# Eight 128 KB weight loads issued in other steps of a linear-attention front end on one core

## The chip, the cores and the metric

The kernel runs on one core of a Trainium2 chip. A core has TensorE (PE in the profile, with its weight loads as PEld), VectorE (DVE), ScalarE (ACT), GpSimd (POOL) and SyncE (SP), and 16 DMA engines that all transfers share. The metric is the device time of one execution in microseconds (us), lower is better; times here are medians over a few executions.

## The reference, cut to what matters

A decayed linear attention over four batches of 768 rows, 8 heads of 64, is followed by a low-rank mixer over the rows and a two-layer feed-forward block.

```python
for b in range(nb):                      # blocks of 64 rows
    intra = np.einsum('bhic,bhjc->bhij', qb, kb) * Dmask[None]
    intra = np.einsum('bhij,bhjd->bhid', intra, vb)
    inter = np.einsum('bhid,bhde->bhie', qb * lam_pow[None], kv_state)
    out[:, :, sl] = intra + inter
    kv_state = lam_block[None, :, None, None] * kv_state + np.einsum('bhsd,bhse->bhde', kb_dec, vb)
# x: the attention output as (batch, row, 512)
h = x.transpose(0, 2, 1) @ U @ V                    # rank 32, over the 768 rows
u = x + h.transpose(0, 2, 1)
out = u + np.maximum(u @ w_ch1, 0.0) @ w_ch2        # 512 -> 2048 -> 512
```

The mixer's weights (U, V, w_ch1, w_ch2) arrive as 64-bit floats. The kernel loads them as pairs of 32-bit words and turns them into 32-bit floats itself.

## The kernel before, in words

**Stages.** The attention takes rows in 24 steps of 128 (NS = 24; six steps, NT = 6, make a batch). After it the first feed-forward product runs over 16 column tiles of w_ch1, and then the second product. Order on every engine is the order in which the code issues, since the whole front part is written out by hand under a manual schedule (L811-L851): for each step s the list `pieces` (L698-L732) names what is issued, and the loop at L838 issues it.

**A step of the attention.** In step s TensorE turns the q and k of step s+1 (`prep`, L416), multiplies the masked scores with v (`intra`, L514), updates the state (`state`, L486), adds the old state's share (`inter`, L525) and makes the scores of step s+1 (`scores`, L463), into which the mixer of an earlier batch is woven (`mix`, L618, and `turn`, L675). ScalarE copies q and k out of PSUM (L422), copies the output (`inter`, L531), scales the state (L456) and splits (L689). VectorE masks the scores (`masked`, L472), adds the mixer's output (`mixed`, L630), splits (L690) and writes the new state (L492, L494, L497). GpSimd scales q and k (L447, L436) and subtracts (L682). At the end of each batch (steps 5, 11, 17) `low` (L541) makes the low-rank product, and in the step after it, the turn of the batch (6, 12, 18), ScalarE and GpSimd split it (L584, L585) and SP exchanges parts of it with four 32 KB transfers (`other`, L595), on which the next `mix` waits.

**Queues.** SP issues the loads of q (in `prep`) and of k (`next_k`), the stores of u (`store`, L646) and the exchange L595; ScalarE issues the loads of v (`next_v`). SP's order in a step is: q load, in a turn of a batch L595 four times, then what `aside` issues, then the store, then the k load. A queue issues in order. The program gives its transfers eight completion semaphores in rotation, over SP's and ScalarE's queues alike, so each issue also waits for the landing of the transfer issued eight earlier.

**The steps of a weight.** `weight_steps` (L133) makes a list of small steps for one weight tile, and `aside(s)` (L800) issues those that a table sets at step s, ahead of `masked(s+1)`. For a tile of w_ch1 loaded in parts (`w1_steps(ft, True, True)`, L221) there are twelve: four fetches, each a 128 KB DMA on SP (L149; 128 rows of 1 KB); `one` (VectorE L170 on all four parts, with two ScalarE operations, L177 and L178, put off to the next step by `on_scalar`); the mantissa (L158); `two` (L188); `three` (L196, which needs L178); `four` (L201); `five` (ScalarE L231); `six` (L234); `seven` (L239). Steps set at NS run after the attention. The converted tiles 0 and 1 are the weights of the first products right behind the attention (L889, L900).

Of the kernel before, what the change touches and what calls it, by code (L numbers as in the profile page):

```python
# [18 lines left out]
def kernel(  # L19
# [40 lines left out]
    NS = B * NT  # L60
# [28 lines left out]
    def on_scalar(what):  # L89
        if late and late[0] is None:  # L90
            late.append(what)
        else:
            what()
# [115 lines left out]
    def plain(keep, key, tag="wf"):  # L209

        def dst():
            if key not in keep:
                keep[key] = (
                    tmp("wg") if tag == "tmp" else
                    plain_pool[-1].tile(
                        [P, C], FP32, tag=tag, bufs=1 if len(plain_pool) == 1 else 3, name="wf"
                    )
                )
            return keep[key]

        return dst  # L221
# [3 lines left out]
    def w1_steps(ft, in_parts=False, apart=False):  # L225
        st = {}

        def five():
            w1v[ft] = o = w_tile(ft)
            st["t"], st["p"] = o[:, 0, :].bitcast(FP32), w1_plain[ft]  # L230
            on_scalar(lambda: nc.scalar.mul(o[:, 0, :], st["p"], NEAR))  # L231

        def six():
            nc.vector.tensor_tensor(  # L234
                out=w1v[ft][:, 1, :], in0=st["p"], in1=st["t"], op=ALU.subtract
            )

        def seven():
            nc.vector.scalar_tensor_tensor(  # L239
                w1v[ft][:, 2, :], st["t"], -E, w1v[ft][:, 1, :].bitcast(FP32), ALU.mult, ALU.add  # L240
            )

        cols = moe_w_ch1[:, ft * P : (ft + 1) * P].rearrange("(c p) f -> p c f", p=P)
        return weight_steps(plain(w1_plain, ft), cols, C, in_parts=in_parts, apart=apart) + [
            five, six, seven,
        ]
# [47 lines left out]
    def w_tile(n):  # L294
        pool = more_w[0] if n > 1 and (n - 2) % 5 < 2 else w1_pool
        return pool.tile([P, 3, C], F32R, tag="w1", name="w1")
# [451 lines left out]
    def v_steps():  # L748

        st = {}  # L750

        def dst():
            if "v" not in st:
                st["v"] = wconv.tile([P, C], FP32, tag="wf", name="vf")[0 : 2 * R, 0:SH]
            return st["v"]

        def parts(gs):
            for half in range(2):
                rows, cols = slice(half * R, (half + 1) * R), slice(half * SH, (half + 1) * SH)
                for g in gs:  # L760
                    yield v_hl[g * R : (g + 1) * R, cols], rows

        def five():
            st["t"] = t = wconv.tile([P, C], FP32, tag="wt", name="vt")[0 : 2 * R, 0:SH]
            nc.vector.tensor_scalar(
                t.bitcast(U32), st["v"].bitcast(U32), HI, None, ALU.bitwise_and
            )
            on_scalar(high)

        def high():  # L770
            for out, rows in parts((0, 2)):
                nc.scalar.copy(out, st["t"][rows])

        def low(g, engine):
            for out, rows in parts((g,)):
                engine.tensor_tensor(
                    out=out, in0=st["v"][rows], in1=st["t"][rows], op=ALU.subtract
                )

        halves = [moe_V[:, half * SH : (half + 1) * SH] for half in range(2)]  # L780
        return weight_steps(dst, halves, SH, 2 * R, in_parts=True) + [
            five, lambda: low(1, nc.vector), lambda: low(3, nc.gpsimd),
        ]
# [6 lines left out]
    for steps, at in (  # L790
        (u_side, (-1, 1, 1, 2, 2)),
        (v_steps(), (0, 0, 3, 3, 4, 4, 4, 5, 5)),
        (w1_steps(0, True, True), (8, 9, 10, 11, 12, 14, 15, 16, 17, 17, 20, 21)),
        (w1_steps(1, True, True), (14, 15, 16, 17, 18, 22, 23, NS, NS, NS, NS, NS)),
    ):
        assert len(steps) == len(at)
        for step, n in zip(steps, at):
            side.setdefault(n, []).append(step)
# [695 lines left out]
```

## Time and profile before

| what | value |
|---|---|
| median of 3 runs | 641.93 us (641.23 to 645.38) |
| the profiled execution's own time | 642.39 us |
| its span, first to last instruction | 640.6 us |
| granted TensorE clock | 0.999 |
| attention, from the first scores to the first L889 product | 6.5 to 115.4 us |
| DMA queues, bytes in the whole span | q1 (SP) 121.53 MB, q10 (ScalarE) 6.42 MB, q8 (instructions) 0.67 MB |

The profile shows one execution. Times in it count from the start of the span. "Share" in a DMA column is the mean busy share of the 16 DMA engines; it can pass 1, as packets of one engine overlap. In the chain that ended last, "issue" is time in which the engine waited for nothing that the profile shows. A row of the timeline gives the start, the duration, the engine, the line and operation, the tiles written and read, and in brackets the idle time before it with what ended it.

### The profile page before, as it was taken

What the parts mean: (1) busy time and instruction counts of PE and PEld (TensorE: products, weight loads), DVE (VectorE), ACT (ScalarE), POOL (GpSimd) and SP (SyncE); (2) the same over time, 40 slices, a digit from 0 to 9 for tenths busy, and PEclk for the clock granted to TensorE, in tenths of its full rate; (3) what the DMA queues carried; (4) which work ended last, traced back from release to release, by engine and by line L of the source; (5) the groups of instructions that cost most, each with busy time, mean ns of one, the idle gap of its engine ahead of it and who ended that gap; (6) DMA issues with size and microseconds to landing.
All of it is one profiled execution on the core that took longest, in us unless ns stands there. A gap on an engine that the chain in (4) does not pass through costs nothing.

```text
span 640.6 us, 13612 instructions
## 1 busy us (share of the span) xinstructions
PE 631.0 (98%) x5203; PEld 530.8 (83%) x5203; DVE 459.5 (72%) x731; ACT 335.1 (52%) x614; POOL 146.4 (23%) x124
## 2 busy tenths in 40 slices
PE   9999989999999999999999999999999999999997
PEld 8889989888888888888888878888888888888886
DVE  6766867757878788788678799785574755855854
ACT  3776757445777777877777745232322322323220
POOL 4475968100000000000377600030120300300300
PEclk9999999999999999999999999999999999999999
DMA  9989996347888798765477786463363363543521
GB/s 218 252 205 266 225 245 161 135 171 269 310 288 273 271 322 290 252 208 202 160 258 231 243 310 222 134 226 99 103 227 98 117 205 100 179 140 99 181 83 65
DMA packets 141379, 128.83 MB, mean 201 GB/s; under 512 B 82498, under 2 KB 99394, under 8 KB 141314
## 3 DMA queue, kind: packets, MB, share of 16 engines
q1 hardware_dynamic: 116192, 121.53, 59.3%
q10 hardware_dynamic: 25122, 6.42, 4.4%
q8 instruction: 41, 0.67, 0.4%
q14 instruction: 24, 0.20, 0.1%
HBM read 78.64 MB, written 48.89 MB: 199 GB/s over the span
## 4 chain that ended last, share of the span: by engine, by line
PE 96%; DMA 2%; DVE 1%; issue 1%; ACT 1%; ACTq 0%; DVEq 0%
PE pz L959 25%; PE pz L1336 14%; PE pz L1334 14%; PE pd L1338 13%; PE z L959 4%; PE pss L463 4%; PE px L514 4%; PE p L959 3%; PE pz L889 2%; PE d L959 2%; PE px L525 2%; PE pqk L416 2%; PE c L959 1%; PE pkv L486 1%; PE pd L900 1%; PE pm L618 1%
## 5 line engine op out<-in xcount | busy, mean ns | idle before, releaser
L1318 ACT ACTIVATE m<-rm 128x512 fp32r<-128x512 f32 x96 | 60.6, 632 | 174.4 <-PE pd L1338 134.2
L1319 DVE SCALAR_TENSOR_TENSOR m<-rm,m 128x512 fp32r<-128x512 f32 x96 | 71.6, 747 | 81.7 <-ACT m L1318 81.7
L959 PE MATMUL pz<-u_hl,w 128*128 128x512 f32 x448 | 110.3, 389 | 0.0
L1334 PE MATMUL pz<-w_hl,m 128*128 128x512 f32 x264 | 102.7, 389 | 0.0
L1336 PE MATMUL pz<-w_hl,m 128*128 128x512 f32 x264 | 102.7, 389 | 0.0
L1338 PE MATMUL pd<-w_d,m 128*128 128x512 f32 (+1 forms) x267 | 101.4, 387 | 0.0
L959 PEld LDWEIGHTS pz<-u_hl,w 128*128 128x128 f32 x448 | 84.1, 188 | 17.5
L285 POOL TENSOR_TENSOR w<-w 128x512 fp32r<-128x512 f32 (+1 forms) x28 | 40.2, 1451 | 213.7 <-DVE w L279 194.3
L1320 DVE SCALAR_TENSOR_TENSOR m<-m 128x512 fp32r<-128x512 f32 x96 | 74.8, 779 | 3.0
L1366 POOL TENSOR_TENSOR o<-o,u 128x512 f32<-128x512 f32 x20 | 29.8, 1517 | 198.9 <-DVE o L1362 198.9
L959 PE MATMUL pz<-u_d,w 128*128 128x512 f32 x224 | 59.7, 389 | 0.0
L1338 PEld LDWEIGHTS pd<-w_d,m 128*128 128x128 f32 x267 | 49.8, 188 | 10.3
L1334 PEld LDWEIGHTS pz<-w_hl,m 128*128 128x128 f32 x264 | 49.6, 188 | 10.4
L1336 PEld LDWEIGHTS pz<-w_hl,m 128*128 128x128 f32 x264 | 49.6, 188 | 10.2
L959 PEld LDWEIGHTS pz<-u_d,w 128*128 128x128 f32 x224 | 42.0, 188 | 8.7
L966 ACT ACTIVATE pz<-pz 128x512 f32<-128x512 f32 x60 | 34.9, 581 | 26.6 <-PE pz L959 26.6
L1336 PE MATMUL pz<-w,m 128*128 128x512 f32 x120 | 46.7, 389 | 0.0
L1334 PE MATMUL pz<-w,m 128*128 128x512 f32 x120 | 46.7, 389 | 0.0
L1338 PE MATMUL pd<-w,m 128*128 128x512 f32 x120 | 46.7, 389 | 0.0
L472 DVE TENSOR_TENSOR sm<-pss,mask 128x512 f32<-128x512 f32 x48 | 30.9, 686 | 20.4 <-PE pss L463 20.4
L970 ACT ACTIVATE r<-pz 128x512 f32<-128x512 f32 x60 | 35.7, 596 | 14.2 <-PE pz L959 12.8
L196 DVE SCALAR_TENSOR_TENSOR sc<-words,sc 128x512 uint32<-128x512 uint32 (+2 forms) x34 | 24.7, 726 | 21.0 <-ACT sc L178 21.0
(144 smaller groups left out, 1112.3 us busy)
## 6 DMA issues: line engine op xcount, KB each, us to landing
r_d<-r SPq DMA_DIRECT2D x96, 256.0 KB, 2.9
rm<-r_d SPq DMA_DIRECT2D x96, 256.0 KB, 2.6
words<-in_moe_w_ch_dram SPq DMA_DIRECT2D x30, 512.0 KB, 4.6
wf<-forms_d SPq DMA_DIRECT2D x53, 128.0 KB, 2.8
u_d<-x_nat SPq DMA_DIRECT2D x24, 256.0 KB, 4.1
u<-u_d SPq DMA_DIRECT2D x24, 256.0 KB, 4.6
qraw<-in_q_dram SPq DMA_DIRECT2D x23, 256.0 KB, 4.8
out_dram<-o SPq DMA_DIRECT2D x23, 256.0 KB, 2.0
```

Of the source, the lines that this page charges most:

```text
L285: engine.tensor_tensor(out=st["third"], in0=st["low"].bitcast(FP32), in1=st["hi"].bitcast(FP32), op=ALU.subtract,)
L472: nc.vector.tensor_tensor(out=sm[:, x], in0=pss[:, x], in1=mask[:, x], op=ALU.mult)
L959: nc.tensor.matmul(out=out, lhsT=weights, rhs=moving, start=start and i == 0, stop=i == len(pieces) - 1, skip_group_check=not start,)
L966: nc.scalar.mul(acc, acc, 1.0 + E)
L970: nc.scalar.mul(r, acc, 4096.0)
L1318: nc.scalar.activation(out=m[:, 0], in_=r, func=AF.Relu, scale=NEAR)
L1319: nc.vector.scalar_tensor_tensor(m[:, 1], r, 0.0, hi, ALU.max, ALU.subtract)
L1320: nc.vector.scalar_tensor_tensor(m[:, 2], hi, E, low, ALU.mult, ALU.subtract)
L1334: nc.tensor.matmul(out=pz, lhsT=m[:, 0, cols], rhs=hi, start=first, stop=False)
L1336: nc.tensor.matmul(out=pz, lhsT=m[:, 1, cols], rhs=low, start=False, stop=end)
L1338: nc.tensor.matmul(out=pd[:, part], lhsT=m[:, 2, cols], rhs=third[:, part], start=first, stop=end, skip_group_check=part.stop != C,)
L1366: nc.gpsimd.tensor_tensor(out=o, in0=o, in1=u, op=ALU.add)
```

## The change

Two rows of the table that sets the steps of tiles 0 and 1 of w_ch1 are changed; nothing else.

```diff
-        (w1_steps(0, True, True), (8, 9, 10, 11, 12, 14, 15, 16, 17, 17, 20, 21)),
-        (w1_steps(1, True, True), (14, 15, 16, 17, 18, 22, 23, NS, NS, NS, NS, NS)),
+        (w1_steps(0, True, True), (6, 7, 11, 12, 13, 14, 15, 16, 17, 17, 20, 21)),
+        (w1_steps(1, True, True), (13, 18, 19, 20, 21, 22, 23, NS, NS, NS, NS, NS)),
```

Tile 0: the four fetches move from steps 8, 9, 10, 11 to 6, 7, 11, 12, and `one` from 12 to 13. Tile 1: the fetches move from 14, 15, 16, 17 to 13, 18, 19, 20, and `one` from 18 to 21. The other steps stay, with the two ScalarE operations of `one` following it, to steps 14 and 22. The number of instructions of every engine is the same (429 rows of SP, 646 of VectorE, 489 of ScalarE in both programs); TensorE's and GpSimd's order is the same throughout.

## The prediction

> **What bounds the kernel now.** I read the page first, then the chain of work that ended last, then the busy time of each engine step by step, then the timelines of SP, VectorE and ScalarE around the steps that change. TensorE is busy nearly all the time, so a word load costs or saves something only where it makes TensorE stop.
>
> ```profile
> PE 631.0 (98%) x5203; PEld 530.8 (83%) x5203; DVE 459.5 (72%) x731; ACT 335.1 (52%) x614; POOL 146.4 (23%) x124
> ```
>
> The chain runs through TensorE's own work from 37.05 to 115.4 us, with these stops in the steps concerned:
>
> ```profile
> 81.34 0.27 PE px L525 x6
> 81.61 0.91 issue
> ...
> 91.67 0.77 issue
> ...
> 106.43 0.41 issue
> ```
>
> The first two lie in steps 16 and 18, inside and just behind the four steps (14 to 17) that load words now; the third, in step 21, does not. TensorE waits there for nothing that the profile shows. The DMA part of the page for 79 to 83 us has one 16 KB packet of the instruction queue, about one per 256 instructions over the whole span (41 packets, 0.67 MB, two times 5203 TensorE instructions). I take these stops to be late instruction packets; that is an inference.
>
> The busy time in stretches that each begin with the scores of a step (issued at the end of the step before) has as its last two columns the DMA share and GB/s. Below are the stretches from the scores of step 13, right behind a turn of a batch; of 15 and 16, with words; of 19, behind the next turn; and of 21.
>
> ```profile
> 63.90:69.13 5.23, 5.04 (x130) 4.62 (x131) 3.69 (x9) 4.97 (x11) 4.92 (x7) 1.00 0.65 152
> ...
> 73.34:77.65 4.31, 4.31 (x125) 4.07 (x125) 4.08 (x7) 3.12 (x8) 4.31 (x4) 1.00 1.10 280
> 77.65:83.19 5.54, 4.63 (x127) 4.29 (x126) 4.16 (x7) 3.06 (x8) 3.87 (x4) 1.00 1.02 258
> ...
> 93.24:98.04 4.80, 4.70 (x129) 4.46 (x130) 3.50 (x9) 4.30 (x8) 4.65 (x6) 1.00 0.68 170
> ...
> 102.25:107.30 5.05, 4.63 (x127) 4.29 (x126) 4.69 (x7) 3.17 (x8) 5.05 (x5) 1.00 0.67 180
> ```
>
> The DMA engines are full in an ordinary step and two thirds full around the turns and in the last steps. The change moves words from full steps to emptier ones. Where it is tight is the turn at step 12: first SP, then VectorE.
>
> ```profile
> 64.11 2.80 SPq L595 DMA_DIRECT2D vp<-vp  x4
> 67.00 0.68 SPq L646 DMA_DIRECT2D u_d<-x_nat  x1
> ```
>
> ```profile
> 69.17 0.69 DVE L630 TENSOR_TENSOR x_nat<-pm,x_nat 128x512 f32<-128x512 f32 x1 [0.64 <-PE pm L618]
> 70.06 1.29 DVE L472 TENSOR_TENSOR sm<-pss,mask 128x512 f32<-128x512 f32 x2 [0.20 <-PE pss L463]
> ```
>
> The last words of tile 0 go out between the two SP rows, at about 66.95. `one`, which needs them, now stands between the two VectorE rows, ahead of the mask that TensorE waits for.
>
> **The change part by part.** No instruction is added or removed; every cost is of place. The sum is against the profiled execution: span 640.6 and 1.8 around it, 642.39 us, which is 0.46 above the median of 641.93.
>
> *Words leave steps 8 to 10 and 14 to 17.* What can go is the 0.91 and the 0.77. The bounds are nothing (the packets are late anyway, as in step 21) and the whole 1.68. If only the packets come sooner, the next things are late. At 81.61: ScalarE waited 3.13 us before its output copy at 84.08, because the v load ahead of it was held till 83.61 by a q load (issued 76.27, with words at 73.28 and 77.13 around it). The copy of k of that step ended at 85.86 + 0.59 = 86.45, and the scores that need it began at 86.92: 0.47 of the 0.91 is to be had even with ScalarE as late as now, and more if q lands sooner. At 91.67: the mix at 97.53 needs the last L595 transfer, issued at 94.98 and landed 2.2 later, at 97.2, so 0.35 of the 0.77. These two give 0.82. I take 1.0, nearer to 0.82 than to 1.68.
>
> *`one` of tile 0 behind the turn.* The words go out at 66.95. When do they land? The eight word loads of before took 4.5 to 7.2 us, all in full steps. In this lull 256 KB of v (issued 63.94) took 3.2 and the last 32 KB of L595 took 2.2. By 3.2 they land at 70.15; VectorE is ready at 69.86, so it waits 0.3. `one` took 0.61 and 0.42 before. The mask then begins at 70.57 to 70.76 instead of 70.06, and its first half (0.69) is done at 71.26 to 71.45. TensorE took it up at 71.17 in the chain, so it loses 0.1 to 0.3. Lower bound 0 (landing by 69.6); upper bound by the slowest row, 66.95 + 7.2 + 0.61 + 0.69 - 71.17 = 4.3. I take 0.3, since the v row is from the same lull. Behind `one` on VectorE stand the mask, the split and the new state, all of which TensorE needs within the step.
>
> *`one` of tile 1 at step 21.* The last words go out behind the k load of 99.19, at about 100.6. By 7.2 they are there at 107.8, by the median of 5.4 at 106.0. VectorE reaches `one` behind L239, at 107.19, and its mask waits for TensorE until 108.44, an idle time of 1.24 that holds the 0.42. Nothing, unless the slowest row holds: then 107.8 + 0.6 against 108.44, still nothing.
>
> *ScalarE's two operations (0.73 + 0.72) move from steps 13 and 19 to 14 and 22.* In step 14 ScalarE waits 1.19 before its output copy at 73.53; 0.26 is left over, and its k copy ends at 76.64 against scores at 77.65. In step 22 it waits 1.08 before 111.62, and the 0.37 left over ends the copy at 112.6, ahead of the products that write px again at 113.54. Nothing in both; without those waits it would be 1.45 each.
>
> *SP and what it is moved past.* In the new steps the store, the k load and the next q load go out later by one word issue, 0.38 in a lull (at 117.17) and up to 2.41 in a full step. The tightest reader is GpSimd's k scaling, which waited 0.57 and 1.39 for k at 82.38 and 86.06, in steps with words. Behind step 12, k landed at 73.0 and is read at 74.00, so 1.0 of slack takes the 0.4 to 0.7. In steps 18 to 20 the q loads have ended or are about to, and GpSimd has no work on the last k. No exchange is moved: all four L595 stand ahead of the words. In the other direction, in steps 8 to 10 and 14 to 17 a transfer that waits for the one eight earlier finds it two steps back instead of 1.6. I take 0.1 for all of this, between 0 and 0.9 (as much as the first stop).
>
> Sum: -1.0 + 0.3 + 0.1 = -0.6, so 641.8 for an execution like the profiled one, and 641.93 - 0.6 = 641.3 for a median of the kind shown.
>
> **What the Trainium skill says against it.** The instruction queue is served beside the full data queues, and the stops came with DMA shares of 1.02 and 1.09. The Trainium skill, "DMA: Bandwidth & Descriptors", section "Queues, rings and completion order", says that each DMA engine goes round between the queue rows it has work for, packet by packet. By that, an instruction packet does not stand behind the words in SP's row, and moving them would not bring it sooner. The trace agrees so far as rows share: from 79 to 83 us the ScalarE queue took 27.9% beside SP's 77.1%. What an instruction packet waits for, no row of before shows. What it would give is the second rival below.
>
> **The rivals.**
>
> 1. *Forecast: the stops shrink, VectorE waits a little.* 641.3. For it: both long stops are in the word steps 14 to 18, the new places have shares of 0.65 to 0.68. Against it: steps 8 to 11 load words at shares of 0.97 to 1.14 and show no stop over 0.1.
> 2. *The stops stay.* They are a matter of when TensorE crosses into a new block, and come back at other steps. Then 641.93 + 0.3 + 0.1 = 642.3. For it: the stop of 0.41 in step 21, with no words near, and steps 8 to 11 without any.
> 3. *Slower: VectorE's wait behind the turn decides.* Place: `one` in step 13. Every us by which the words land after 69.9 delays the mask, and from about 70.1 TensorE with it. By the fastest old row, 4.5, they land at 71.45; TensorE then gets its mask at 71.45 + 0.5 + 0.69 = 72.6, 1.5 late; by the median 5.4, 2.4 late. With the gain of 1.0 that is 641.93 - 1.0 + 1.5 to 2.4 + 0.1 = 642.5 to 643.4, and slower than before from a landing of about 70.9 on. Against it: the DMA share of 0.65 and the 3.2 of v.
> 4. *Everything goes: all three stops (2.09), no wait.* 639.8.
>
> **How the numbers follow.** The forecast has 0.45, the second rival 0.25, the third 0.2, the fourth 0.1. The predicted time is 641.3. Three of the executions shown lie within 1.2 us of each other and one 3.5 above; so I put about 1 us around the cases. From 640.0 (short of the fourth) to 643.6 (the third by the median row) leaves out 2 in 10. For the likeliest alone it is 640.5 to 642.3. One per cent is 6.4 us, about what a measurement of this kernel can tell from no change. The idle time of TensorE in all stretches from 37.05 to 115.40 us adds up to 2.8, so no gain of that size can be had here, and a loss of that size takes the third rival's upper bound of 4.3 in more than one place. Faster by over 1% 0.01, within 1% 0.97, slower by over 1% 0.02.
>
> **What would show it.** Right: the chain has no issue row near 0.8 in steps 14 to 18; VectorE's L170 in step 13 shows an idle time of some 0.3 before it that ends with the words' landing; the step from the scores of 14 to those of 15 keeps about 4.2 to 4.5 us; words issued in step 12 land in about 3 us. Wrong: issue rows of the same sum elsewhere (second rival), or L170 in step 13 idle for over 1 us with L514 behind it late (third). I would also be wrong if the moved words brought a stop to steps 18 to 21, where I count only 0.1.

## The result, and the profile after

| what | before | changed |
|---|---|---|
| median of 22 runs each | 641.36 us (639.07 to 645.38) | 643.98 us (641.41 to 647.96) |
| the profiled execution, and its span | 642.39, 640.6 us | 645.23, 643.4 us |
| first scores of step 7 to the first L889 product | 37.05 to 115.40: 78.35 us | 37.61 to 118.21: 80.60 us |
| from there to the end of the span | 525.2 us | 525.2 us |

The changed kernel is slower: the ratio of the times is 1.0034, with a 95% interval of 1.0020 to 1.0048, some 2.2 us (1.3 to 3.1). That is within the 1% band of the chances, but on the other side from the forecast and above the range (643.6). Of the 2.8 us between the profiled executions 0.6 arises ahead of step 7, where little has been moved yet, 2.2 in the rest of the attention, and nothing behind it. So the steps concerned are where to look.

The busy line of the page of the changed kernel is almost the one of before, with the same counts of instructions; TensorE's own work has not grown.

```profile
PE 631.3 (98%) x5203; PEld 530.6 (82%) x5203; DVE 460.8 (72%) x731; ACT 334.7 (52%) x614; POOL 146.2 (23%) x124
```

The chain that ended last (start, length, what) now has two issue stops and two detours over other engines, where before, from 37.05 on, it had TensorE alone. The first detour runs over ScalarE, GpSimd and SP's four L595 to the words, the second over SP's words and k load to ScalarE:

```profile
59.02 0.76 issue
...
68.66 3.25 DMA words<-in_moe_w_ch_dram
...
72.38 0.69 DVE sm L472
...
87.95 1.61 issue
...
99.49 5.25 DMA kraw<-in_k_dram
104.85 0.37 ACTq L337
```

The issue stops are 0.76 + 1.61 = 2.37, against 0.91 + 0.77 + 0.41 = 2.09. They have not gone: the longest stands in step 17, from which the words were taken. The detours end in TensorE's stops, which its timeline shows in brackets:

```profile
73.21 1.19 PE L514 MATMUL px<-vraw,sm 128*64 128x64 f32 x32 [0.47 <-DVE sm L472]
...
109.14 1.13 PE L463 MATMUL pss<-qt,kt 64*128 64x128 f32 x15 [0.15 <-DVE kv L494]
...
112.03 1.24 PE L514 MATMUL px<-vraw,sm 128*64 128x64 f32 x32 [0.75 <-ACT qt L422]
```

Those are 0.47 + 0.15 + 0.75 = 1.37 of new stops. With a fourth of 0.28 at 98.33, and 0.28 more of issue stops, it is 1.9 of the 2.2; the other 0.3 lies in no single stop. (The fourth is not the change's: two later profiles of the kernel before have 0.28 at the same L486 too.) Each of the three rows has its cause on another engine. A stop is named below by the step in which TensorE issues what comes late: a wait of VectorE ahead of the mask, in step 13, is a stop of L514 in step 14.

*Words late in step 13, the stop in step 14 (73.21).* SP's timeline, then VectorE's:

```profile
65.97 2.63 SPq L595 DMA_DIRECT2D vp<-vp  x4
68.66 0.58 SPq L149 DMA_DIRECT2D words<-in_moe_w_ch_dram  x1
```

```profile
72.03 0.43 DVE L170 TENSOR_SCALAR sc<-words 128x512 uint32<-128x512 uint32 x1 [0.59 <-DMA words<-in_moe_w_ch_dram]
72.38 1.28 DVE L472 TENSOR_TENSOR sm<-pss,mask 128x512 f32<-128x512 f32 x2
```

`one` idles 0.59 until the words land, 3.3 after their issue. The mask stands behind it.

*`one` in step 21, the stop in step 22 (112.03).* VectorE, then GpSimd:

```profile
108.91 0.99 DVE L239 SCALAR_TENSOR_TENSOR w<-w 128x512 fp32r<-128x512 f32 x1
109.83 1.50 DVE L170 TENSOR_SCALAR sc<-words 128x512 uint32<-128x512 uint32 x1
111.25 1.28 DVE L472 TENSOR_TENSOR sm<-pss,mask 128x512 f32<-128x512 f32 x2
```

```profile
109.32 1.74 POOL L682 TENSOR_TENSOR u_d<-u_hl 128x512 fp32r<-128x512 f32 x1
```

Here the words, issued at 106.01, landed 3.6 later, just before `one` began, so no wait shows. The same operation takes 1.50 instead of 0.43, and ends at 111.33, 0.27 after GpSimd's subtraction (109.32 + 1.74 = 111.06). The first half of the mask then ends at 111.25 + 0.69 = 111.94, and L514 starts 0.1 later, at 112.03. The releaser that its row names, a copy of ScalarE, ended at 111.97, so this row alone does not tell the two apart; but in the four other profiles with this stop L514 starts 0.1 behind the mask's first half as well, and in one21_only the copy named had ended 0.20 before. Before, the same place looked like this on VectorE and GpSimd:

```profile
108.44 1.29 DVE L472 TENSOR_TENSOR sm<-pss,mask 128x512 f32<-128x512 f32 x2 [1.24 <-PE pss L463]
```

```profile
106.61 1.71 POOL L682 TENSOR_TENSOR u_d<-u_hl 128x512 fp32r<-128x512 f32 x1
```

VectorE's idle 1.24 from 107.19 on was there, and GpSimd's subtraction stood in it till 108.32. By the 0.28 with which `one` ends behind GpSimd, an estimate puts its end at 108.60, behind the mask's start.

*The v load of step 20, the stop of the scores issued in step 21 (109.14).* ScalarE, and its row of before:

```profile
104.85 0.37 ACTq L337 DMA_DIRECT2D vraw<-in_v_dram  x1
105.32 0.59 ACT L531 COPY x_nat<-px 128x512 f32<-128x512 f32 x1 [1.74 <-DMA kraw<-in_k_dram]
```

```profile
102.32 0.59 ACT L531 COPY x_nat<-px 128x512 f32<-128x512 f32 x1 [1.07 <-PE px L525]
```

ScalarE does not need this k. Its v load waits on the completion semaphore that the k load of step 18 (issued 99.49) uses, and everything of ScalarE behind the v load is 1.74 late; the state and the scores follow. Before, the transfer eight earlier was the last of the short exchange L595, landed some 4 us ahead, and the copy waited for TensorE alone. No run changes the rotation alone; this cause is read from the traces.

### The profile page after: what moved, and what is told of

Same layout as the page of the kernel before. It is cut to its first block, busy times and chain, and to the rows that moved or that the text cites. A ratio compares the mean times of both kernels' runs of the same rounds, so it can differ in the third digit from the quotient of the medians.

```text
span 643.4 us, 13607 instructions
## 1 busy us (share of the span) xinstructions
PE 631.3 (98%) x5203; PEld 530.6 (82%) x5203; DVE 460.8 (72%) x731; ACT 334.7 (52%) x614; POOL 146.2 (23%) x124
## 4 chain that ended last, share of the span: by engine, by line
PE 92%; DMA 3%; ACT 2%; issue 1%; DVE 1%; SPq 0%; ACTq 0%; POOL 0%; DVEq 0%
PE pz L959 25%; PE pz L1334 14%; PE pz L1336 14%; PE pd L1338 13%; PE z L959 4%; PE p L959 3%; PE pss L463 3%; PE px L514 3%; PE pz L889 2%; PE d L959 2%; PE px L525 2%; PE c L959 1%; DMA kraw<-in_k_dram 1%; PE pqk L416 1%; PE pd L900 1%
## 5 line engine op out<-in xcount | busy, mean ns | idle before, releaser
L472 DVE TENSOR_TENSOR sm<-pss,mask 128x512 f32<-128x512 f32 x48 | 30.9, 685 | 21.3 <-PE pss L463 21.3
```

The lines of the kernel that those rows point to most:

```text
L472: nc.vector.tensor_tensor(out=sm[:, x], in0=pss[:, x], in1=mask[:, x], op=ALU.mult)
```

## The experiments

Theory A: the loss is made of these waits, and each belongs to a place: the words behind the turn, GpSimd's work beside `one`, and the rotation of semaphores; the issue stops come and go by themselves. Theory B, the rival: the issue stops make the difference. They depend on the word loads, moving those has made stops elsewhere, and the waits of A are covered by slack in other steps. Times of the kernels below have intervals of 1.1 to 2.1 us either way, as wide as what is looked for, so the verdicts rest on the stops in the traces, and the ratios are only told. All edits are to the table of the two rows if no other line is shown, each run has one profile, and a kernel not said to be the changed one starts from the kernel before.

### One part at a time

```diff
 one21_only:  tile 1  (14, 15, 16, 17, 18, 22, ...) -> (14, 15, 16, 17, 21, 22, ...)
 one13_only:  tile 0  (8, 9, 10, 11, 12, 14, ...)   -> (8, 9, 10, 11, 13, 14, ...)
 tile0_only:  tile 0  -> (6, 7, 11, 12, 13, 14, ...)
 tile1_only:  tile 1  -> (13, 18, 19, 20, 21, 22, ...)
```

> The kernel before, with only `one` of tile 1 moved from step 18 to 21; all fetches stay where they were, so no words are late. Theory A (the added time comes from where `one` now stands on VectorE): L170 in step 21 runs beside a GpSimd operation and takes 1 to 1.5 us instead of 0.42, the mask of step 22 and TensorE's L514 behind it are 0.5 to 1.0 late: +0.5 to +1.0 us. Theory B (it comes from the words' new places in the DMA queues, by later instruction packets): 0, L170 hidden in VectorE's idle 1.24.

> The kernel before, with only `one` of tile 0 moved from step 12 to 13; fetches unchanged, the last words land at about 63 and `one` stands at about 70, so it has nothing to wait for. Theory A: 0 to +0.4 (a stretch beside GpSimd at most; the wait of 0.59 on words of the changed kernel is not there). Theory B: 0.

> Only the row of tile 0 is changed (fetches in 6, 7, 11, 12 and `one` in 13). Theory A: VectorE waits about 0.6 for words in step 13 and TensorE stops for about 0.5: +0.5 to +0.8. Theory B: by issue stops alone, an unknown part of the 2.2 us; no stop in step 13 needed.

> Only the row of tile 1 is changed (fetches in 13, 18, 19, 20 and `one` in 21). Theory A: ScalarE's v load of step 20 waits over 1 us for a landing, L170 of step 21 is stretched, and TensorE stops for about 0.9 in steps 21 and 22: +0.9 to +1.6. Theory B: +0 to +2.2, in issue stops.

| kernel | ratio to before (95%) | attention from step 7, us | stop of L514, step 14 | of L463, step 21 | of L514, step 22 |
|---|---|---|---|---|---|
| one21_only | 1.0017 (0.9999 to 1.0034) | 78.1 | 0 | 0 | 0.88 |
| one13_only | 1.0007 (0.9987 to 1.0028) | 79.4 | 0 | 0 | 0 |
| tile0_only | 1.0010 (0.9988 to 1.0032) | 78.3 | 1.59 | 0 | 0 |
| tile1_only | 1.0016 (0.9988 to 1.0043) | 81.2 | 0 | 0.55 | 0.56 |

In one21_only no load is moved, only `one` of tile 1. GpSimd's, VectorE's and TensorE's timelines:

```profile
109.59 1.73 POOL L682 TENSOR_TENSOR u_d<-u_hl 128x512 fp32r<-128x512 f32 x1
```

```profile
110.11 1.50 DVE L170 TENSOR_SCALAR sc<-words 128x512 uint32<-128x512 uint32 x1
```

```profile
112.30 0.89 PE L514 MATMUL px<-vraw,sm 128*64 128x64 f32 x20 [0.88 <-ACT qt L422]
```

`one` ends 0.29 after the subtraction (111.61 and 111.32), as in the changed kernel. So this stop comes with the place of `one`, without any word load near. For step 13, one13_only and tile0_only differ by the place of the loads alone. VectorE's row in each:

```profile
70.39 0.49 DVE L170 TENSOR_SCALAR sc<-words 128x512 uint32<-128x512 uint32 x1
```

```profile
72.91 0.56 DVE L170 TENSOR_SCALAR sc<-words 128x512 uint32<-128x512 uint32 x1 [1.59 <-DMA words<-in_moe_w_ch_dram]
```

With the last load in step 11 there is no wait; with it in step 12, `one` waits 1.59 for words that landed 4.3 after their issue at 68.46. Tile1_only brings the wait at the semaphore back, in ScalarE's row:

```profile
105.02 0.59 ACT L531 COPY x_nat<-px 128x512 f32<-128x512 f32 x1 [2.02 <-DMA kraw<-in_k_dram]
```

Tile1_only shows one thing more about step 21: there, as in after_again and after_early_last below, `one` first waited for its words too. Its row in after_again:

```profile
108.37 0.82 DVE L170 TENSOR_SCALAR sc<-words 128x512 uint32<-128x512 uint32 x1 [0.60 <-DMA words<-in_moe_w_ch_dram]
```

The waits were 0.59, 0.60 and 0.71, for words that SP issued at 103.2 to 104.5 and that landed 4.3 to 5.5 later. They did not set the price: `one` then took 0.71 to 0.83 and ended 0.28 behind GpSimd's subtraction again, which had begun ahead of it.

Each stop appears with its part and without the others, as A has it. B keeps a point: the attention of tile0_only took no longer than before in spite of 1.59, because its issue stops in steps 14 to 18 were 0.2 and not 1.7.

### The changed kernel, mended at one place and at both

```diff
 after_early_last:  tile 0 of the changed kernel  (6, 7, 11, 12, 13, ...) -> (6, 7, 11, 11, 13, ...)
 after_one23:       tile 1 of the changed kernel  (13, 18, 19, 20, 21, 22, 23, ...) -> (13, 18, 19, 20, 23, 23, 23, ...)
 after_both:        both of these;  after_both_2: the same again, on another chip
 after_again:       the changed kernel itself, beside after_both_2
```

> The changed kernel, with the last fetch of tile 0 taken from step 12 to 11, so that its words land before `one` in step 13. Theory A (the cost sits where `one` stands): no idle time before L170 in step 13 and no stop of L514 behind it; the stop in step 22 stays: against the kernel before +0.9 to +1.6 us. Theory B (the cost is later instruction packets by the words' new places): as the changed kernel, +2.2.

> The changed kernel, with the first three VectorE operations of tile 1 (L170, L158, L188) all in step 23, behind the last mask; all fetches as in the changed kernel. Theory A: the stop in step 22 (0.75 in the changed kernel, 0.88 with `one` alone moved) is gone, the wait for words in step 13 stays: +0.5 to +1.3 us against the kernel before. Theory B: +2.2. If words of step 20 are what held step 22, the stop goes too.

> Both edits at once: the changed kernel with tile 0's last fetch in step 11 and tile 1's three VectorE operations in step 23. Nearly all word loads are at the new places. Theory A: 0 to +0.4 us against the kernel before. Theory B: still +2.2, in issue stops.

> The changed kernel with tile 0's last fetch in step 11 and tile 1's VectorE operations in step 23, repeated beside the changed kernel. Theory A: 0 to +0.5 against the kernel before and 1.5 to 2 below the changed one. Theory B: as the changed one.

> The changed kernel once more, on the chip and among the runs of the next one: +1.5 to +2.9 us against the kernel before, a wait for words in step 13 and a stretched L170 in step 21. Its issue stops are a second sample: about 2 us by theory A (no matter of the change), and not less.

| kernel | ratio to before (95%) | attention from step 7, us | words' wait in step 13 | stop of L514, step 14 | of L463, step 21 | of L514, step 22 |
|---|---|---|---|---|---|---|
| changed kernel | 1.0034 (1.0020 to 1.0048) | 80.5 | 0.59 | 0.47 | 0.15 | 0.75 |
| after_again | 1.0016 (0.9995 to 1.0037) | 78.9 | 0.56 | 1.53 | 0.67 | 0.55 |
| after_early_last | 1.0015 (0.9984 to 1.0047) | 78.1 | 0 | 0.24 | 0.45 | 0.55 |
| after_one23 | 1.0013 (0.9986 to 1.0039) | 80.8 | 1.74 | 2.65 | 0 | 0 |
| after_both | 1.0002 (0.9975 to 1.0029) | 78.6 | 0 | 0.32 | 0.20 | 0 |
| after_both_2 | 1.0012 (0.9993 to 1.0032) | 77.2 | 0 | 0.40 | 0 | 0 |

The columns for steps 13, 14 and 22 follow the edits. after_again shows why the stop in step 14 can be three times the words' wait. Its GpSimd, VectorE and TensorE:

```profile
70.39 2.69 POOL L682 TENSOR_TENSOR u_d<-u_hl 128x512 fp32r<-128x512 f32 x2
```

```profile
70.41 1.53 DVE L170 TENSOR_SCALAR sc<-words 128x512 uint32<-128x512 uint32 x1 [0.56 <-DMA words<-in_moe_w_ch_dram]
```

```profile
72.69 1.19 PE L514 MATMUL px<-vraw,sm 128*64 128x64 f32 x32 [1.53 <-DVE sm L472]
```

GpSimd's subtraction starts 0.02 ahead of `one`, and `one` takes 1.53. In the first profile of the changed kernel `one` was first, took 0.43, and the subtraction behind it took 1.49. So the late words cost twice: by the wait, and by bringing `one` into GpSimd's work. Without the words' wait (after_both_2) part of the second stays. VectorE's row, then GpSimd's:

```profile
69.49 1.04 DVE L170 TENSOR_SCALAR sc<-words 128x512 uint32<-128x512 uint32 x1
```

```profile
69.19 1.07 POOL L436 TENSOR_TENSOR ks<-kraw,small 128x512 f32<-128x512 f32 x1
```

Here it is not the subtraction but the scaling of k (L436) that `one` meets, and it ends 0.27 behind that. So the loss is not bound to L682: with its words in time, `one` in step 13 still cost 0.24 to 0.40 in three profiles, and nothing in one13_only, where it took 0.49.

Two expectations were missed. after_again came to 1.0 us by its ratio, not 1.5 to 2.9, with 0.35 us of issue stops instead of 2; and after_both_2, among the same runs, is 0.3 below it by the ratios, not 1.5 to 2. The times do not show the mend, the stops do.

Both mends together leave no kernel that beats before. One reason shows behind the attention: with three VectorE steps of tile 1 in step 23, the part from the first L889 product to the end of the span is 525.9 to 526.0 us in six profiles, against 525.2 to 525.4 in all kernels with those steps in 22 or earlier. That is 0.6 or 0.7 given back.

### GpSimd's subtraction moved out of the way

If GpSimd's subtraction is what stretches `one` in step 21, moving it must cure step 22 with `one` left in step 21. `turned` of 13 (L682) goes ahead of `turned` of 14 in the list of pieces:

```diff
 one21_only, and:
+    pieces.remove(("turned", 13))
+    pieces.insert(pieces.index(("turned", 14)), ("turned", 13))
```

> `one` of tile 1 alone in step 21, as in an earlier run, and GpSimd's L682 of step 21 put off to step 22, so that no GpSimd operation runs while L170 does. Theory A in its sharper form (L170 started inside a GpSimd operation ends 0.28 after that operation's end, so GpSimd's end sets it): L170 takes about 0.42, L514 of step 22 does not stop for it, and the 0.9 us of `one` alone in step 21 go: 0 to +0.3 against the kernel before. If the stretch of L170 has another cause, it stays near 1.5 and the time stays at about +0.9.

> Repeat of the kernel with `one` of tile 1 in step 21 and GpSimd's L682 of step 21 put off. Its order on TensorE gains nothing by itself: 0 +- 0.6 against the kernel before; the first median of -0.6 and the attention of 76.5 us without any issue stop were chance, unless they come again.

Ratios 0.9989 (0.9968 to 1.0010) and 1.0003 (0.9979 to 1.0027). The stop of L514 in step 22 is 0 in both. GpSimd and VectorE in the first:

```profile
104.12 1.27 POOL L447 TENSOR_TENSOR qs<-qt,powq 128x512 f32<-128x512 f32 x1
108.42 1.28 POOL L447 TENSOR_TENSOR qs<-qt,powq 128x512 f32<-128x512 f32 x1 [3.03 <-ACT qt L422]
```

```profile
105.90 0.42 DVE L170 TENSOR_SCALAR sc<-words 128x512 uint32<-128x512 uint32 x1
106.73 1.29 DVE L472 TENSOR_TENSOR sm<-pss,mask 128x512 f32<-128x512 f32 x2 [0.41 <-PE pss L463]
```

GpSimd is idle from 105.39 to 108.42, `one` takes its 0.42, and the mask waits for TensorE, as the prediction had counted it. That settles the price of step 21: it is GpSimd's operation beside it. It is a repair of the edit, no gain over before.

### Do the word loads make the issue stops?

The forecast's gain rests on this. In the first kernel below tile 1's words leave steps 14 to 17 without any of the new waits of steps 13 and 21; in double_words they are loaded a second time in steps 8 to 11; late_words is tile1_late with the VectorE steps in 22 and the subtraction moved.

```diff
 tile1_late, _b, _c:  tile 1  -> (20, 20, 21, 21, 23, 23, 23, ...)
 double_words:  tile 1's four fetches also at (8, 9, 10, 11), ahead of (14, 15, 16, 17, 18, 22, ...)
 late_words:    tile 1  -> (20, 20, 21, 21, 22, 22, 23, ...), and ("turned", 14) ahead of ("turned", 15)
 before_b, before_c:  the kernel before, for two more profiles
```

> The kernel before, with tile 1's four fetches in steps 20, 20, 21, 21, when the loads of q and k have ended, and its three VectorE operations in step 23; steps 12 to 19 load no words. This asks for the gain that the prediction counted: if words in full steps make the instruction packets late, the issue stops of steps 14 to 18 go and the time falls by 1.0 to 1.7 us. If they have nothing to do with them, 0, with issue stops of about 2 us in all somewhere in the attention.

> The kernel without words in steps 12 to 19 again (0.58 us of issue stops in steps 14 to 18 in its first profile). If words cause them: under 0.6. If not: as spread as in the kernel before.

> As the run before it: under 0.6 if words cause the stops, 0 to 2 if not.

> The kernel before again, for its issue stops in steps 14 to 18 (1.68 us in the first profile). If words in full steps cause them: 1 to 2 us again. If they are a matter of the single execution: anything from 0 to 2.

> As the run before it: 1 to 2 us of issue stops in steps 14 to 18 if words cause them, 0 to 2 if not.

> The kernel before, with tile 1's four word loads issued once more in steps 8 to 11 (the same data, loaded again in steps 14 to 17), so that steps 8 to 11 load 256 KB of words each. If words in full steps make instruction packets late, as the prediction's main gain took it, issue stops of 0.8 or more appear in steps 8 to 12, where the kernel before has none, and the time rises by 0.8 to 2 us. If not, 0 to +0.3, with TensorE running on.

> The kernel before, with tile 1's fetches in steps 20, 20, 21, 21, L170 and L158 of it in step 22 and L188 in 23, and GpSimd's L682 of step 22 put off to step 23. If words in steps 14 to 17 cost about 0.7 in issue stops, and L170 and L158 fit into VectorE's idle time of step 22 when no GpSimd operation runs beside them: the attention takes 77.5 to 78.2 us, the rest 525.3, and the time is 0.5 to 1.0 below that of the kernel before. If the gain is chance: 0, and if L170 is stretched again, a stop of 0.5 to 0.9 in step 23.

Ratios: tile1_late 1.0005 (0.9973 to 1.0037), double_words 1.0026 (1.0003 to 1.0050), late_words 0.9999 (0.9980 to 1.0018); the kernels executed once gave 649.08 (tile1_late_b, which reaches step 7 some 6 us later than tile1_late), 642.08 (tile1_late_c), 643.03 and 642.49 (before_b, before_c). TensorE's waits at L525, from 73 to 100 us, and in tile1_late_b, which starts 6 us later, from 79 to 106 (what it waited for, total, times, longest), in before_b, before_c, tile1_late, tile1_late_b and tile1_late_c:

```profile
PE px L525 <- issue: 1.8, 2, 1.3
```

```profile
PE px L525 <- issue: 1.1, 1, 1.1
```

```profile
PE px L525 <- issue: 0.6, 1, 0.6
```

```profile
PE px L525 <- issue: 1.1, 1, 1.1
```

```profile
PE px L525 <- issue: 0.3, 1, 0.3
```

The ranges overlap: 1.7, 1.8 and 1.1 with the words there, 0.6, 1.4 (the 1.1 and 0.3 at L514) and 0.3 without. Over all profiles, the issue stops of steps 14 to 18 add up to 0.99 us on average in the eight with words in steps 14 to 17 (0 to 1.9; double_words, with 1.7, apart) and 0.76 in the eleven without (0 to 2.4). So the words may be worth some 0.2 there, by the scatter with an uncertainty of about 0.7 either way. The closest pair, three profiles of before against three of tile1_late, has 1.5 against 0.8, and attentions of 78.7 against 77.9. That difference of 0.8 is the 0.82 of the prediction's sum, but three profiles of a kind with stops of 0.3 to 1.8 do not tell it from nothing, and behind the attention tile1_late gives 0.6 back. So the gain of 1.0 is neither shown nor excluded. Double_words does not decide it either: its time rose by 1.7 us, as expected if words make stops, but TensorE's issue stops in steps 8 to 12 are 0.6 and not 0.8 or more, where before_b and before_c had 0.5 and 0.3. Its longest stop, 1.67, stands in step 17, which loads what it loaded before.

B is thus not borne out as the cause of the loss: from step 7 to the end of the attention the issue stops add up to 2.7 and 0.35 in the two profiles of the changed kernel, and to 2.4, 2.9 and 2.1 in the three of before. It is right in that the issue stops, at 0 to 2.4 us in steps 14 to 18 from execution to execution, scatter as much as what is looked for. Late_words missed its aim: its attention took 79.5, not 77.5 to 78.2, with issue stops of 1.5 in steps 8 to 12. Besides, the subtraction that was moved ran at once after GpSimd's scaling of q and met the mantissa step (L158), which took 1.50 and ended 0.29 behind it; TensorE's L514 stopped for 0.37. That gave back more than half of the 0.6 that the earlier place had won. GpSimd's row:

```profile
113.89 1.50 POOL L682 TENSOR_TENSOR u_d<-u_hl 128x512 fp32r<-128x512 f32 x1
```

## Why the prediction was wrong, point by point

- **`one` of tile 0 behind the turn, +0.3: right place, too small.** This is the term that failed most. TensorE lost 0.47, 1.53, 1.59 and 2.65 in the four profiles with the last load in step 12, 1.6 on average. Two terms were mis-sized. The landing was put at 3.2, by the row of v; it took 3.3, 3.4, 4.3 and 4.4, and `one` waited 0.56 to 1.74 instead of 0.3. And `one` was given 0.42 to 0.61; in three of the four it began within GpSimd's subtraction, and took 0.56, 1.47 and 1.53. The 0.61 of before had the same cause: that `one` (64.28) began within an operation of GpSimd (L585) and ended 0.29 behind it. The third rival named this place and, for a landing of 4.5, a price of 1.5.
- **`one` of tile 1 at step 21, 0: failed.** VectorE's idle time of 1.24 was there, but `one` ended 0.28 behind GpSimd's subtraction and not 0.42 after its start. The step looked at VectorE's queue and at the landing, and not at what GpSimd does in the same microsecond, which a row of before shows. Price 0.55 to 0.88 in five profiles, 0 with GpSimd's subtraction moved or with `one` in step 23. No rival had it. The landing was wrong as well: the words were to go out at about 100.6, as if the words of steps 18 and 19 did not stand ahead of them on SP; they went out at 103.2 to 106.0 in the four profiles with this step's load and `one` in step 21, and in three of these `one` waited for them.
- **SP and what it is moved past, +0.1: too small.** The scores issued in step 21 came 0.15, 0.67, 0.55, 0.45 and 0.20 late in five of the seven profiles with a word load in each of the steps 18 to 20, and not late in the other two: 0.3 on average. The step counted the issues that stand behind a word load on SP, and followed the rotation of semaphores only for the steps that lose loads. Where loads are added, the v load of step 20 comes to wait for a full k load instead of a 32 KB one. The prediction did say that a stop in steps 18 to 21 would show it wrong.
- **Words leave steps 8 to 10 and 14 to 17, -1.0: not borne out, its size open.** The step assumed that the 0.91 and the 0.77 belong to the words of those steps. In the first profile of the changed kernel there is 1.61 in step 17, and the issue stops add up to 2.37 instead of 2.09; in the second there is none in steps 14 to 18. The kernel before in three profiles has 1.7, 1.8 and 1.1 there: one profile was read as a fixed pattern. Over nineteen profiles the words account for 0.2, in the closest pair for 0.8, and neither is told from 0. The second rival ("the stops stay") is not excluded; the 0.41 of step 21 and the quiet steps 8 to 11, both quoted against the forecast, had pointed to it. (One reading in the step is slightly off: the last L595 was issued at 95.04 and not at 94.98, so 0.29 and not 0.35 of the 0.77 was to be had.)
- **ScalarE's two operations, 0: nothing against it.** No stop in step 14 or 22 of the changed kernel ends with L177 or L178.
- **The sum.** With the measured sizes: 0 to -0.8 for the issue stops, 1.6 for step 14, 0.65 for step 22 and 0.3 for step 21 make 1.8 to 2.6, beside the 2.2 (1.3 to 3.1) of the ratio. So the costs, put at 0.4 and measured at 2.6, turn the sign whatever the gain was. The attention of the two profiles of the changed kernel (80.5 and 78.9) is only 1.0 longer than that of the three of before (78.3, 79.3, 78.5), since after_again had no issue stop in steps 14 to 18. In the three profiles with a stop of 1.5 or more in step 14 those issue stops were only 0, 0.2 and 0.4. Whether a long wait makes the issue stops fewer, no experiment tested; after_early_last and one21_pool_later had none there without such a wait. Nor is it known what an instruction packet waits for.

The range ended at 643.6, just above the third rival, which has the gain of 1.0 still in it (643.4). The cases were taken as alternatives, while the second and the third can hold together: stops that stay, and a wait behind the turn.

The question put under "What the Trainium skill says against it", whether packets of instructions stand behind words, stays open: moving the words did not bring them reliably sooner, which is what that rule would give, but the scatter is too wide for a verdict.

## What to carry to other kernels

When an operation of VectorE is moved into an idle gap, read GpSimd's timeline at the new place as well as the gap: an operation of 0.42 us did not fit into 1.24 because GpSimd was at work there. When a transfer is added to queues that share completion semaphores in rotation, write down for each later issue which transfer it now waits for. And take a stop that is given as "issue" as a gain only after it has stood at the same place in several profiles.

## What the runs showed of the hardware

- A VectorE `tensor_scalar` over 128x512 words (L170) took 0.42 us alone and up to 1.53 where it began within a `tensor_tensor` of GpSimd (L682, L436 or L585); it then ended 0.27 to 0.29 after GpSimd's. The other way round, GpSimd's L682 took 1.46 to 1.50 where it began within L170 and 1.71 to 1.75 within L239, but its usual 1.28 to 1.31 within the mask L472. The Trainium skill, "SBUF — State Buffer", section "Who interferes with whom", says that VectorE in its two-port mode and GpSimd shut each other out for the whole instruction, whichever begins first. The trace agrees, by these rows and by the 0.42 that came back when L682 was moved; in which mode L170 ran, no row shows.
- A 128 KB word load behind a turn (DMA share 0.65 to 0.71 over the stretch at step 13) took 3.3 to 4.4 us to land there, though 256 KB of v took 3.2 in that stretch of the kernel before; the one in step 18 of the changed kernel took 2.3. A lull on average says little about one transfer.
- The issue stops of TensorE in steps 14 to 18 added up to 0 to 2.4 us over the profiles of these kernels, and to 0 and 1.6 in two of the changed kernel alone.
